# Windowed attention and a gated feed-forward in one kernel: sixteen steps ordered by hand instead of eleven, a bias added by TensorE, two decoding instructions a step

## The chip, the cores and the metric

One core of one Trainium2 chip. The metric is the device time of one execution in microseconds (us).

## The reference, cut to what matters

```python
# q, k, v: (4, 8, 768, 64) float32; n_global = 8, n_local = 96 (int64 inputs)
scores = (1 / sqrt(64)) * q @ k^T
keep   = (key < n_global) | (0 <= query - key < n_local)
dist   = n_local where a key is only global, else |query - key|
scores = where(keep, scores - slope[head] * dist, -1e9)      # slope = 2 ** -(head + 1)
x      = softmax(scores) @ v        # heads side by side: (4, 768, 512)
h      = relu(x @ w_in)             # w_in (512, 1024), float64
c      = h conv_w over 3 neighbours in the sequence
out    = (h * sigmoid(c)) @ w_out   # w_out (1024, 512), float64
```

The weights of the feed-forward arrive as float64 and are decoded on the chip from their two words.

## The kernel before, in words

**Attention.** A job is one batch, one half of the sequence (384 queries) and one pair of heads: 4 x 2 x 4 = 32 jobs of 3 steps of 128 queries, 96 steps. A step sees at most 232 keys (96 before it, its own 128, 8 global ones). `scores` (L371) multiplies q and k into PSUM. For jobs 0 to 8 (`NATIVE` = `BESIDE` = 9) these are float32 matmuls over 64 rows, and the two heads of the pair stand in rows 0 to 63 and 64 to 127; head 0 writes a tile `s`, head 1 a tile `sb` of another pool (banks m0, m1). From job 9 on q is split into a high and a low part (`prep`, L125) and both heads write one tile `s`. `maxima` (L403) adds the table of biases with one VectorE instruction a head, scales by -0.125 and takes the minimum; its result goes back into PSUM. `exps` (L418) is ScalarE's exponential with its sum, and a small ScalarE instruction (L431) that adds an offset to the sum. `normalise` (L433) is a step later: a reciprocal on VectorE, head 0 on GpSimd, head 1 on ScalarE while `s < SHARED`. `transposes` (L445), two steps later, turns the probabilities by TensorE and moves them out by ScalarE (L453). `values` (L456) multiplies a job's three steps by v, and `mixed` (L477) splits the result into xh (ScalarE, L481) and xl (VectorE, L482).

**Feed-forward.** `ffn(n)` (L647) lists the work of half a batch: `mm1` (x @ w_in, L489), `relu`, `conv` (one GpSimd and two VectorE instructions, L539), `gate`, `saturated`, `split`, and `mm2` (L604). It is queued when a half's four jobs are through (every 12 steps) and spread over the steps that follow.

**Decoding.** A piece of the weights is 512 words a partition; there are 16, w_in first. Each needs three VectorE instructions on its words (`weight_bits`, L310), a GpSimd cast (`weight_high`, L321) and one VectorE subtraction (`weight_low`, L326). `work` takes them off a list while a budget in us a step lasts; their listed costs are 0.35, 0.62, 0.62 and 0.56. `need` forces pieces that a matmul is about to read. A piece that has been read out frees the buffer of the load four pieces later.

**Order.** Steps 0 to `HAND` - 1 = 10 run in the program's order on every engine, with a few warm-up matmuls between (`WARM`). From step 11 on a scheduler orders each engine's instructions at build time from its own estimate of when operands and buffers come free. The eight PSUM banks are: two `s`, two for transposes, one for values, and m0, m1, m2.

The loop of the steps by hand (L774 on), before:

```python
scores(s)
if ends(s - LAG_V): values((s - LAG_V) // NB)
transposes(s - LAG_T)          # with ScalarE's eviction
maxima(s); exps(s); normalise(s - 1)
# tables of the next heads, warm-up matmuls
work("dve", budget)
if ends(s - LAG_V - 1): mixed((s - LAG_V - 1) // NB)
work("pool", 1.3)
# loads; prep of the next job where i == 0
```

Of the kernel before, what the change touches and what calls it, by code (L numbers as in the profile page):

```python
# [20 lines left out]
P = 128  # L21
# [14 lines left out]
NPB = 3  # L36
SHARED = 40
CHECK_EVERY = 3
HAND = 11
NATIVE = 9  # L40
BESIDE = 9
WARM = (43, 0, 12, 0, 0, 8, 8, 4, 4, 4, 4, 4)
WARM_INSIDE = (0, 0, 14, 8, 8)
EARLY = 1
DECODE_BY_HAND, DECODE_LATER = (0.3, 1.2, 1.4), (1.2, 1.2)
FIRST_LOADS = (0, 0, 1, 2)
SHARE = (0.3, 0.5)
AT = ((2, 4, 5, 9, 16, 25), (1, 2, 4, 6, 7, 12, 16))
# [18 lines left out]
def fast_path(tc, io):  # L67
# [49 lines left out]
    def load_v(m):  # L117
# [32 lines left out]
    load(0)  # L150
    load(1)

    turns = [0, 0]

    def bank(name, scores=False):
        s = cur.get("s", 0)
        own = (2,) if s < NB * BESIDE else (0,) if exact else (0, 1, 2)
        if scores:
            own = (0, 1)
        turns[scores] += 1  # L160
        k = own[turns[scores] % len(own)]
        return ps_m.tile([P, 512], F32, tag=f"m{k}", name=name)
# [208 lines left out]
    def scores(s):  # L371
        m, i = steps[s]
        b, u, hp = jobs[m]
        w = NKC[u]
        first = u == 0 and i == 0
        n, c0 = (W0, NPREV) if first else (WIN, 0)
        k0 = key_start(u, i)
        both = ps_s.tile([P, 2, 256], F32, tag="s", name=f"s{s}")
        sp = [both[:, 0], bank(f"sb{s}", True) if m < BESIDE else both[:, 1]]
        for j in range(2):  # L380
            if m < NATIVE:
                rq, rk = raw[m]
                r, a = (j * D, 0) if m < BESIDE else (0, j)
                last_mm[s] = T.matmul(  # L384
                    sp[j][:, c0 : c0 + n],
                    rq[r : r + D, a * TB + i * P : a * TB + (i + 1) * P],
                    rk[r : r + D, a * w + k0 : a * w + k0 + n],
                    start=True,
                    stop=True,
                )  # L390
                continue
            qh, ql, kk = qk[m]
            for n_, (q_, st, sp_) in enumerate(((qh, True, False), (ql, False, True))):
# [7 lines left out]
        st_s[s] = (sp, c0, n, first)  # L401

    def maxima(s):  # L403
        m, i = steps[s]
        b, u, hp = jobs[m]
        sp, c0, n, first = st_s[s]
        mm = p1.tile([P, 8], F32, tag="mm", name=f"mm{s}", bufs=6)
        for j in range(2):
            h = 2 * hp + j
            tb = tab[:, h, WIN:] if first else tab[:, h, 0:WIN]  # L410
            last_ttr[s] = V.tensor_tensor_reduce(  # L411
                out=sp[j][:, c0 : c0 + n], in0=sp[j][:, c0 : c0 + n], in1=tb,
                scale=-0.125, scalar=3.0e38, op0=ALU.add, op1=ALU.min,
                accum_out=mm[:, j : j + 1],
            )
        st_s[s] = (sp, c0, n, mm)
# [28 lines left out]
    def transposes(s):  # L445
        m, i = steps[s]
        pb, _, _, _ = st_s.pop(s)
        pt = ps_t.tile([P, 2, 2, P], F32, tag="t", name=f"t{s}")
        for j in range(2):
            for c in range(2):  # L450
                T.transpose(pt[:, j, c, :], pb[:, j, c * P : (c + 1) * P], ident)  # L451
        sb = p2.tile([P, 2, 2, P], F32, tag="pt", name=f"pt{s}", bufs=NB + 1)
        last_ev[s] = A.activation(sb, pt, AF.Copy)  # L453
        st_pt[s] = sb

    def values(m):  # L456
# [17 lines left out]
                    stop=c == 1,  # L474
                )

    def mixed(m):  # L477
# [4 lines left out]
        cur["mixed"] = V.tensor_tensor(xl, pv[m], xh.bitcast(F32), ALU.subtract)  # L482

    def ends(s):
        return s >= 0 and s % NB == NB - 1
# [285 lines left out]
    for s in range(len(steps) + LAG_V + 1):  # L771
        cur["s"] = s
        m, i = steps[s] if s < len(steps) else (len(jobs), -1)
        if s < HAND:  # L774
# [2 lines left out]
                values((s - LAG_V) // NB)  # L777
            if s < len(WARM_INSIDE):
                warm(WARM_INSIDE[s])
            if s >= LAG_T:  # L780
                transposes(s - LAG_T)
            maxima(s)
            exps(s)
            if s:
                normalise(s - 1)
            if i == 1 and m + 1 < NPAIR:
                table(2 * m + 2, X=G)
                table(2 * m + 3, X=G)
# [8 lines left out]
                conv_weights((s - 4) // 2)  # L797
            budget = DECODE_BY_HAND[min(s // 3, len(DECODE_BY_HAND) - 1)]
            work("dve", budget)
            if ends(s - LAG_V - 1):  # L800
                mixed((s - LAG_V - 1) // NB)
            work("pool", 1.3)
        else:
            if hand:
# [14 lines left out]
                    left += 1  # L819
                k = -(-sum(cost for cost, _, _ in queue) // left)  # L820
            if ends(e):
                mixed(e // NB)
            if s <= len(steps):
                normalise(s - 1)
            if s < LAG_V + SPU:
# [125 lines left out]
    def general_head(m, hp, i, j, qg, kg, vg, dist, mask, parts):  # L951
# [94 lines left out]
```

## Time and profile before

| what | us |
|---|---|
| three runs | 463.18, 462.77, 453.68 |
| median of the runs | 462.77 |
| the profiled execution | 452.65 |
| its span, first to last instruction | 450.73 |

| engine | busy us in the span |
|---|---|
| TensorE | 434.5 |
| VectorE | 351.9 |
| ScalarE | 304.0 |
| GpSimd | 225.8 |

Busy time is the sum of an engine's instructions in the profiled execution. The records call TensorE PE, its weight loads PEld, VectorE DVE, ScalarE ACT, GpSimd POOL; L411 is line 411 of the kernel. Times in a row count from the start of the span. Matmuls are pipelined and their ends are modelled, so that their spacing from start to start says more than their length.

### The profile page before, as it was taken

The numbers are of one execution on the slowest core, as the hardware profiler recorded it, in microseconds if no ns is written. First come the engines' busy times: TensorE is split into PE (matmuls) and PEld (weight loads), VectorE is DVE, ScalarE is ACT, GpSimd is POOL, SyncE is SP. The second block draws the span as 40 slices with busy tenths as digits, with TensorE's granted clock in tenths as the row PEclk, the third lists the DMA queues.
The fourth block names the chain that finished last, engine by engine and source line by source line (L and its number), as shares of the span: only waits on it lengthen the run. The fifth ranks groups of instructions, "written<-read, shape, count | busy, mean of one in ns | idle before, by whom it ended". The sixth has DMA issues, their size and how long they took to land.

```text
span 450.7 us, 9020 instructions
## 1 busy us (share of the span) xinstructions
PE 434.5 (96%) x3027; PEld 375.6 (83%) x3027; DVE 351.9 (78%) x927; ACT 304.0 (67%) x839; POOL 225.8 (50%) x315
## 2 busy tenths in 40 slices
PE   8789999999889999999999999999999999998997
PEld 6555678899768988899989988889989988798876
DVE  6899998889989877757989897847989986447800
ACT  3778878788799667647776576646775696547610
POOL 5654446637835472656675585646675651022000
PEclk9989999999999999999999999999999999999999
DMA  6979941343244332353234333442335223584111
GB/s 213 306 221 275 279 121 43 108 147 105 83 129 150 108 107 97 92 166 107 86 120 160 107 108 91 130 138 81 106 119 163 81 83 119 207 293 132 47 49 52
DMA packets 22662, 60.02 MB, mean 133 GB/s; under 512 B 3024, under 2 KB 5584, under 8 KB 22608
## 3 DMA queue, kind: packets, MB, share of 16 engines
q1 hardware_dynamic: 18992, 53.01, 38.1%
q10 hardware_dynamic: 3616, 6.36, 3.8%
q8 instruction: 26, 0.43, 0.4%
q14 instruction: 28, 0.23, 0.2%
HBM read 53.07 MB, written 6.29 MB: 132 GB/s over the span
## 4 chain that ended last, share of the span: by engine, by line
PE 73%; DVE 5%; ACT 4%; DMA 4%; POOL 2%; issue 2%; ACTq 0%; POOLq 0%; DVEq 0%
PE o L611 24%; PE h L500 24%; PE pv L469 7%; PE t L451 7%; PE s L394 6%; DMA check<-in_w 3%; DVE c L547 1%; PE last L632 1%; POOL pbuf L443 1%; PE sb L384 1%; PE s L384 1%; DVE c L548 1%; DVE c L599 1%; ACT pbuf L425 1%; ACT sat L577 1%
## 5 line engine op out<-in xcount | busy, mean ns | idle before, releaser
L443 POOL TENSOR_SCALAR pbuf<-pbuf,mm 128x232 f32<-128x232 f32 (+1 forms) x152 | 109.1, 726 | 74.1 <-DVE mm L437 49.2
L425 ACT ACTIVATE pbuf<-s,mm 128x232 f32<-128x232 f32 (+1 forms) x165 | 72.5, 444 | 37.6 <-DVE mm L411 22.8
L411 DVE CUSTOM_DVE_ANT_0 s<-s,tab 128x232 f32<-128x232 f32 (+1 forms) x165 | 63.1, 384 | 24.9 <-PE s L394 21.8
L546 POOL TENSOR_SCALAR c<-hbuf,cw 128x382 f32<-128x382 f32 (+1 forms) x64 | 50.0, 786 | 59.3 <-ACT hbuf L510 59.3
L611 PE MATMUL o<-woh,gh 128*128 128x512 f32 x184 | 74.0, 402 | 0.0
L611 PE MATMUL o<-wol,gh 128*128 128x512 f32 x184 | 73.2, 398 | 0.0
L611 PE MATMUL o<-woh,gl 128*128 128x512 f32 x184 | 73.2, 399 | 0.0
L451 PE MATMUL t<-ident,pbuf 128*128 128x128 f32 x384 | 63.0, 278 | 6.6 <-ACT pbuf L441 3.7
L453 ACT ACTIVATE pt<-t 128x512 f32<-128x512 f32 x96 | 58.0, 604 | 15.4 <-PE t L451 15.3
L451 PEld LDWEIGHTS t<-ident,pbuf 128*128 128x128 f32 x384 | 45.5, 141 | 19.6 <-ACT pbuf L441 5.1
L500 PE MATMUL h<-xh,wih 128*128 128x384 f32 x252 | 58.1, 345 | 1.7 <-ACT hbuf L510 1.2
L500 PE MATMUL h<-xl,wih 128*128 128x384 f32 x252 | 58.8, 342 | 0.0
L500 PE MATMUL h<-xh,wil 128*128 128x384 f32 x252 | 56.3, 340 | 0.0
L469 PE MATMUL pv<-pt,v 128*64 128x128 f32 (+1 forms) x768 | 50.0, 279 | 0.3 <-ACT pt L453 0.3
L469 PEld LDWEIGHTS pv<-pt,v 128*64 128x64 f32 (+1 forms) x768 | 42.3, 138 | 8.9 <-issue 2.5
L500 PEld LDWEIGHTS h<-xh,wih 128*128 128x128 f32 x252 | 42.9, 189 | 4.1 <-ACT hbuf L510 1.9
L547 DVE SCALAR_TENSOR_TENSOR c<-hbuf,cw,c 128x382 f32<-128x382 f32 (+1 forms) x64 | 43.7, 697 | 3.0 <-POOL c L546 2.7
L500 PEld LDWEIGHTS h<-xh,wil 128*128 128x128 f32 x252 | 44.2, 189 | 0.3 <-issue 0.3
L500 PEld LDWEIGHTS h<-xl,wih 128*128 128x128 f32 x252 | 44.0, 189 | 0.2 <-issue 0.2
L548 DVE SCALAR_TENSOR_TENSOR c<-hbuf,cw,c 128x382 f32<-128x382 f32 (+1 forms) x64 | 43.4, 686 | 0.3
L510 ACT ACTIVATE hbuf<-h 128x384 f32<-128x384 f32 x64 | 31.9, 500 | 17.4 <-PE h L500 17.0
L611 PEld LDWEIGHTS o<-woh,gl 128*128 128x128 f32 x184 | 34.7, 188 | 7.7 <-issue 0.2
(119 smaller groups left out, 846.6 us busy)
## 6 DMA issues: line engine op xcount, KB each, us to landing
v<-in_vv SPq DMA_DIRECT2D x32, 384.0 KB, 3.7
rq<-in_qk SPq DMA_DIRECT2D x23, 384.0 KB, 3.1
wr<-in_w SPq DMA_DIRECT2D x16, 512.0 KB, 5.2
check<-in_w SPq DMA_DIRECT2D x16, 512.0 KB, 4.6
rk<-in_qk SPq DMA_DIRECT2D x12, 504.0 KB, 3.6
out<-ob ACTq DMA_DIRECT2D x23, 256.0 KB, 2.1
rk<-in_qk SPq DMA_DIRECT2D x11, 408.0 KB, 3.2
rq<-in_qk SPq DMA_DIRECT2D x16, 96.0 KB, 4.4
```

The source lines that it names most:

```text
L411: last_ttr[s] = V.tensor_tensor_reduce(out=sp[j][:, c0 : c0 + n], in0=sp[j][:, c0 : c0 + n], in1=tb, scale=-0.125, scalar=3.0e38, op0=ALU. ...
L425: last_exp[s] = A.activation(pb[:, j, c0 : c0 + n], sp[j][:, c0 : c0 + n], AF.Exp, bias=mm[:, j : j + 1], scale=-1.0, accum_out=mm[:, 2 + ...
L443: G.tensor_scalar(x, x, inv, 1.0, ALU.mult, ALU.mult)
L451: T.transpose(pt[:, j, c, :], pb[:, j, c * P : (c + 1) * P], ident)
L453: last_ev[s] = A.activation(sb, pt, AF.Copy)
L469: T.matmul(pv[m][64 * j : 64 * j + 64, i * P : (i + 1) * P], vt[m][:n, i, c, 64 * j : 64 * j + 64], sb[:n, j, c, :], start=c == 0, stop=c ...
L500: T.matmul(ps[:, :TB], w_[:, k, fs], x_, start=part == 0 and k == 0, stop=part == 2 and k == NK - 1,)
L510: A.activation(half, ps[:, :TB], AF.Relu, scale=0.5)
L546: G.tensor_scalar(c, *tap(1), 1.0, ALU.mult, ALU.mult)
L547: V.scalar_tensor_tensor(c, *tap(0), c, ALU.mult, ALU.add)
L548: V.scalar_tensor_tensor(c, *tap(2), c, ALU.mult, ALU.add)
L611: last = T.matmul(ps, g_[:, f], w_[:, f], start=f == 0 and part == 0, stop=f == NF - 1 and part == 2,)
```

## The change

Steps 0 to 15 are ordered by hand instead of 0 to 10, in a new order: ScalarE's high half of the mixed heads comes ahead of the step's exponentials, its eviction of the transposes behind them, VectorE's low half ahead of the decoding. Jobs 1 to 12 (steps 3 to 38) are "biased": q is scaled by -0.125 beforehand, on GpSimd (in place for jobs 1 to 8, in place of the cast for 9 to 12), TensorE adds -0.125 times the table of biases to the scores by a matmul with a bf16 identity, one a head, and VectorE takes the minimum of both heads with one tensor_reduce. Jobs 0 to 8 have one PSUM tile of two banks for both heads, two of them; at job 9 this pool is given up for the old `s`, m0 and m1. The decoding budgets become 0.3 for steps 0 to 2, 0.9 for steps 3 to 15, and 1.2 later.

```diff
-HAND = 11
+HAND = 16
+BIASED = (1, 13)
-DECODE_BY_HAND, DECODE_LATER = (0.3, 1.2, 1.4), (1.2, 1.2)
+DECODE_BY_HAND, DECODE_LATER = (0.3, 0.9), (1.2,)
...
-    ps_s = pool("ps_s", 2, space=PSUM)
-    ps_m = pool("ps_m", 1, space=PSUM)
+    ps_m = {2: pool("ps_m", 1, space=PSUM)}
+    ps_w = tc.tile_pool(name="ps_w", bufs=2, space=PSUM)
+    wide = [ps_w, ps_w.__enter__()]
+    def narrow():
+        wide[0].__exit__(None, None, None)
+        ps = tc.tile_pool(name="ps_s", bufs=1, space=PSUM)
+        ps_s.append(ps.__enter__())
+        ps_m[0] = ps_m[1] = ps_s[0]
...
     def prep(m, part):
+        if m < NATIVE and biased(m) and part == 0:
+            q = raw[m][0][:, :TB]
+            G.tensor_scalar(q, q, -0.125, 1.0, ALU.mult, ALU.mult)
...
-            G.tensor_copy(qh, rq)
+            if biased(m):
+                G.tensor_scalar(qh, rq, -0.125, 1.0, ALU.mult, ALU.mult)
+            else:
+                G.tensor_copy(qh, rq)
...
-            V.tensor_tensor(ql, rq, qh.bitcast(F32), ALU.subtract)
+            if biased(m):
+                V.scalar_tensor_tensor(ql, rq, -0.125, qh.bitcast(F32), ALU.mult, ALU.subtract)
+            else:
+                V.tensor_tensor(ql, rq, qh.bitcast(F32), ALU.subtract)
...
+    A.activation(ident16, ident, AF.Copy, scale=-0.125)
...
-        both = ps_s.tile([P, 2, 256], F32, tag="s", name=f"s{s}")
-        sp = [both[:, 0], bank(f"sb{s}", True) if m < BESIDE else both[:, 1]]
+        if m < BESIDE:
+            both = wide[1].tile([P, 2, 512], F32, tag="s", name=f"s{s}")
+        else:
+            if not ps_s:
+                narrow()
+            both = ps_s[0].tile([P, 2, 256], F32, tag="s", name=f"s{s}", bufs=2)
+        sp = [both[:, 0], both[:, 1]]
+        def bias(j):
+            last_mm[s] = T.matmul(
+                sp[j][:, c0 : c0 + n], ident16, bias_of(s, j), start=False, stop=True
+            )
...
+            if biased(m):          # jobs 9 to 12, behind each head
+                bias(j)
+        for j in range(2 if m < NATIVE and biased(m) else 0):
+            bias(j)                # jobs 1 to 8, behind both heads
...
     def maxima(s):
+        if biased(m):
+            last_ttr[s] = V.tensor_reduce(
+                mm[:, 0:2], both[:, :, c0 : c0 + n], axis=mybir.AxisListType.X, op=ALU.min,
+            )
-        for j in range(2):
+        for j in range(0 if biased(m) else 2):
...
+            x = (s - LAG_V - 1) // NB if ends(s - LAG_V - 1) else None
             if s >= LAG_T:
                 transposes(s - LAG_T)
+            if x is not None:
+                mixed_high(x)
             maxima(s)
             exps(s)
+            if s >= LAG_T:
+                evict(s - LAG_T)
             if s:
                 normalise(s - 1)
+            if x is not None:
+                mixed_low(x)
...
             work("dve", budget)
-            if ends(s - LAG_V - 1):
-                mixed((s - LAG_V - 1) // NB)
             work("pool", 1.3)
```

## Rows read from the trace of the kernel before

**Rows 1.** Busy time by stage: stretch, its length, then for each engine its busy us and (instructions); last the granted clock of TensorE as a share of full, the share of the DMA engines, and GB/s.

```profile
11.75:46.04 34.29, 28.78 (x230) 19.60 (x227) 32.87 (x112) 26.71 (x94) 19.16 (x27) 0.95 0.93 268
46.04:82.00 35.96, 35.88 (x255) 27.81 (x255) 33.45 (x96) 28.33 (x89) 20.64 (x28) 1.00 0.52 159
82.00:140.00 58.00, 53.83 (x397) 47.44 (x398) 52.09 (x117) 49.05 (x141) 31.74 (x34) 1.00 0.34 109
140.00:430.00 290.00, 288.83 (x1962) 257.85 (x1961) 225.42 (x574) 193.05 (x502) 147.84 (x198) 1.00 0.38 121
```

**Rows 2.** VectorE in order of time, the first bias instruction of step 3 and of step 16: start us, length us, engine, line, operation, out<-in, shapes, count.

```profile
11.75 0.31 DVE L411 CUSTOM_DVE_ANT_0 s<-s,tab 128x136 f32<-128x136 f32 x1 [0.29 <-PE sb L384]
...
46.04 0.40 DVE L411 CUSTOM_DVE_ANT_0 s<-s,tab 128x232 f32<-128x232 f32 x1
```

**Rows 3.** The chain of waits between 42 and 82 us: shares of that stretch by line (the chain enters it at 44.74 us).

```profile
by line: PE h L500 33.3%; PE pv L469 14.7%; PE t L451 13.9%; PE sb L384 13.2%; PE s L384 13.0%; PE h L521 3.6%; ACT hbuf L510 1.3%; issue 0.2%
```

**Rows 4.** The chain of waits between 96 and 116 us, some of its pieces.

```profile
98.58 1.22 DVE c L599
...
100.69 3.13 DMA rq<-in_qk
...
105.69 1.41 POOL pbuf L443
```

**Rows 5.** VectorE in order of time, steps 7 and the start of 8.

```profile
24.11 0.40 DVE L411 CUSTOM_DVE_ANT_0 s<-s,tab 128x232 f32<-128x232 f32 x1
...
24.43 0.44 DVE L411 CUSTOM_DVE_ANT_0 sb<-sb,tab 128x232 f32<-128x232 f32 x1
...
24.78 0.16 DVE L437 RECIPROCAL mm<-mm 128x2 f32<-128x2 f32 x1
24.86 0.67 DVE L330 TENSOR_TENSOR wil<-w,wih 128x512 fp32r<-128x512 f32 x1
...
27.07 0.56 DVE L482 TENSOR_TENSOR xl<-pv,xh 128x384 fp32r<-128x384 f32 x1 [0.47 <-ACT xh L481]
```

**Rows 6.** VectorE's instructions by stage (busy us, count, then clock, DMA share, GB/s): first those that read the raw words (tile wr; the two stages), then those of line 330 (the low planes).

```profile
11.75:46.04 34.29, 17.44 (x28) 0.95 0.93 268
46.04:82.00 35.96, 12.77 (x18) 1.00 0.52 159
...
11.75:46.04 34.29, 5.56 (x8) 0.95 0.93 268
```

**Rows 7.** A short reduce on VectorE (groups by form: busy us, mean ns, idle before).

```profile
L358 DVE TENSOR_REDUCE misc<-misc 128x1 f32<-128x32 f32 x1 | 0.2, 178 | 0.0
```

**Rows 8.** TensorE in order of time: the warm-up matmuls (bf16, 128 columns) ahead of the next piece, and two of the score matmuls of a job with split q.

```profile
11.55 0.62 PE L169 MATMUL warm<-setup 128*128 128x128 bf16 x8
12.01 0.39 PE L451 MATMUL t<-ident,pbuf 128*128 128x128 f32 x2
...
86.11 0.27 PE L394 MATMUL s<-kk,qh 128*128 128x232 f32 x1
86.22 0.28 PE L394 MATMUL s<-kk,ql 128*128 128x232 f32 x1
```

**Rows 9.** TensorE in order of time: the scores of a step by hand, and those of a step that the scheduler ordered.

```profile
16.80 0.46 PE L384 MATMUL s<-rk,rq 64*128 64x232 f32 x1
16.81 0.46 PE L384 MATMUL sb<-rk,rq 64*128 64x232 f32 x1
...
17.40 0.33 PE L451 MATMUL t<-ident,pbuf 128*128 128x128 f32 x1
...
48.55 0.66 PE L384 MATMUL s<-rk,rq 64*128 64x232 f32 x2
49.14 0.66 PE L451 MATMUL t<-ident,pbuf 128*128 128x128 f32 x4
49.73 0.66 PE L384 MATMUL sb<-rk,rq 64*128 64x232 f32 x2
```

**Rows 10.** ScalarE in order of time, step 7.

```profile
24.57 0.60 ACT L453 ACTIVATE pt<-t 128x512 f32<-128x512 f32 x1 [0.53 <-PE t L451]
25.06 0.45 ACT L425 ACTIVATE pbuf<-s,mm 128x232 f32<-128x232 f32 x1
...
25.49 0.46 ACT L425 ACTIVATE pbuf<-sb,mm 128x232 f32<-128x232 f32 x1
...
26.07 0.29 ACT L431 ACTIVATE mm<-mm,misc 128x2 f32<-128x2 f32 x1
26.27 0.39 ACT L441 ACTIVATE pbuf<-pbuf,mm 128x136 f32<-128x136 f32 x1
26.57 0.47 ACT L481 ACTIVATE xh<-pv 128x384 fp32r<-128x384 f32 x1
```

**Rows 11.** GpSimd, groups by form: a scaling of 382 columns and a cast of 768.

```profile
L546 POOL TENSOR_SCALAR c<-hbuf,cw 128x382 f32<-128x382 f32 x32 | 24.3, 762 | 18.1 <-ACT hbuf L510 18.1
L137 POOL CAST qh<-rq 128x768 fp32r<-128x768 f32 x23 | 23.2, 1007 | 31.0 <-issue 13.2 <-PE s L394 9.3 <-DMA rq<-in_qk 8.4
```

**Rows 12.** Who waited for whom (us in total, times, longest): the first row of 11.75 to 46.04 us, and the first of 82 to 140 us.

```profile
ACT pt L453 <- PE t L451: 6.2, 10, 1.6
...
POOL qh L137 <- DMA rq<-in_qk: 8.4, 2, 7.1
```

**Rows 13.** The stretch from 20 to 30 us, columns as in Rows 1.

```profile
20.00:30.00 10.00, 8.22 (x74) 6.11 (x74) 9.42 (x30) 7.91 (x28) 5.98 (x8) 0.83 0.87 268
```

More of the change, by code (lines that the diff above doesn't have):

```diff
@@ L82, in fast_path @@
     pg = pool("pg", 4)
-    ps_s = pool("ps_s", 2, space=PSUM)
     ps_t = pool("ps_t", 2, space=PSUM)
     ps_v = pool("ps_v", 1, space=PSUM)
-    ps_m = pool("ps_m", 1, space=PSUM)
+    ps_m = {2: pool("ps_m", 1, space=PSUM)}
     p2 = pool("p2", 2)
+    ps_w = tc.tile_pool(name="ps_w", bufs=2, space=PSUM)
+    wide = [ps_w, ps_w.__enter__()]
+    ps_s = []
+    def narrow():
[3 more added lines that the diff above has]
+        ps_m[0] = ps_m[1] = ps_s[0]
+        pools.insert(len(pools) - 1, ps)
     jobs = [(b, u, hp) for b in range(B) for u in range(2) for hp in range(NPAIR)]
@@ L123, in load_v, with biased @@
         vt[m] = t
+    def biased(m):
+        return BIASED[0] <= m < BIASED[1]
     def prep(m, part):
+        if m < NATIVE and biased(m) and part == 0:
+            q = raw[m][0][:, :TB]
+            G.tensor_scalar(q, q, -0.125, 1.0, ALU.mult, ALU.mult)
         if m >= len(jobs) or m < NATIVE:
@@ L151, in fast_path, with bank @@
     load(1)
-    turns = [0, 0]
-    def bank(name, scores=False):
+    turns = [0]
+    def bank(name):
         s = cur.get("s", 0)
         own = (2,) if s < NB * BESIDE else (0,) if exact else (0, 1, 2)
[L158 to L162, printed above, removed]
+        turns[0] += 1
+        k = own[turns[0] % len(own)]
+        return ps_m[k].tile([P, 512], F32, tag=f"m{k}", name=name)
     queue, cur, exact = [], {}, []
@@ L192, in fast_path @@
     make_identity(nc, ident)
+    ident16 = const.tile([P, P], BF16, name="ident16")
     V.tensor_copy(rel, reli)
@@ L388, in scores @@
                     start=True,
-                    stop=True,
+                    stop=not biased(m),
                 )
@@ L392, in scores @@
             qh, ql, kk = qk[m]
-            for n_, (q_, st, sp_) in enumerate(((qh, True, False), (ql, False, True))):
+            for n_, (q_, st, sp_) in enumerate(((qh, True, False), (ql, False, not biased(m)))):
                 last_mm[s] = T.matmul(
@@ L400, in scores, with bias_of @@
                 )
-        st_s[s] = (sp, c0, n, first)
+            if biased(m):
+                bias(j)
+        for j in range(2 if m < NATIVE and biased(m) else 0):
+            bias(j)
+        st_s[s] = (sp, c0, n, both)
+    def bias_of(s, j):
+        m, i = steps[s]
+        b, u, hp = jobs[m]
+        if u == 0 and i == 0:
+            return tab[:, 2 * hp + j, WIN:]
+        return tab[:, 2 * hp + j, 0:WIN]
     def maxima(s):
@@ L405, in maxima @@
         b, u, hp = jobs[m]
-        sp, c0, n, first = st_s[s]
+        sp, c0, n, both = st_s[s]
         mm = p1.tile([P, 8], F32, tag="mm", name=f"mm{s}", bufs=6)
-        for j in range(2):
-            h = 2 * hp + j
-            tb = tab[:, h, WIN:] if first else tab[:, h, 0:WIN]
+        if biased(m):
[3 more added lines that the diff above has]
+        for j in range(0 if biased(m) else 2):
             last_ttr[s] = V.tensor_tensor_reduce(
-                out=sp[j][:, c0 : c0 + n], in0=sp[j][:, c0 : c0 + n], in1=tb,
+                out=sp[j][:, c0 : c0 + n], in0=sp[j][:, c0 : c0 + n], in1=bias_of(s, j),
                 scale=-0.125, scalar=3.0e38, op0=ALU.add, op1=ALU.min,
@@ L451, in transposes, with evict @@
                 T.transpose(pt[:, j, c, :], pb[:, j, c * P : (c + 1) * P], ident)
+        st_pt[s] = pt
+    def evict(s):
         sb = p2.tile([P, 2, 2, P], F32, tag="pt", name=f"pt{s}", bufs=NB + 1)
-        last_ev[s] = A.activation(sb, pt, AF.Copy)
+        last_ev[s] = A.activation(sb, st_pt[s], AF.Copy)
         st_pt[s] = sb
@@ L475, in block, with mixed_high @@
                 )
-    def mixed(m):
+    def mixed_high(m):
         xh = px.tile([P, TB], F32R, tag="xh", name=f"xh{m}")
@@ L481, in mixed, with mixed_low @@
         A.activation(xh, pv[m], AF.Copy)
-        cur["mixed"] = V.tensor_tensor(xl, pv[m], xh.bitcast(F32), ALU.subtract)
+    def mixed_low(m):
+        xh, xl = xt[m]
+        V.tensor_tensor(xl, pv[m], xh.bitcast(F32), ALU.subtract)
     def ends(s):
@@ L821, in fast_path @@
             if ends(e):
-                mixed(e // NB)
+                mixed_high(e // NB)
+                mixed_low(e // NB)
             if s <= len(steps):
@@ L832, in fast_path @@
                 transposes(s - LAG_T)
+                evict(s - LAG_T)
             fill(k - k0)
@@ L957, in general_head @@
         for c, (a, z) in enumerate(parts):
-            sp = ps_s.tile([P, 512], F32, tag="s", name=f"gs{t}_{c}")
+            sp = ps_s[0].tile([P, 512], F32, tag="s", name=f"gs{t}_{c}", bufs=2)
             T.matmul(
```

## The prediction

> **What bounds the kernel now.** I read the busy times by stage first [rows 1]. From 11.75 to 46.04 us, which are steps 3 to 15 (the first bias of step 3 starts at 11.75, that of step 16 at 46.04 [rows 2]), VectorE is busy 32.87 of 34.29 us, ScalarE 26.71, TensorE 28.78. That stage is VectorE's: 34.29 / 13 = 2.64 us a step. From 46.04 to 82 TensorE is busy 35.88 of 35.96 us. From 82 to 140 VectorE has 52.09 and ScalarE 49.05 of 58 us; from 140 to 430 TensorE has 288.83 of 290. A busy TensorE is not TensorE at its peak, so I checked with the chain of waits: from where it enters the second stage, at 44.74, to 82 it is TensorE's but for 1.5% of the stretch [rows 3], while between 97 and 116 us it goes through VectorE's gate products, the load of one rq and the scalings on GpSimd [rows 4]. After 140 us nothing of the change runs, so I carry that stage over as it is.
>
> What a hand-ordered step costs VectorE is read in its order of time [rows 5]: at step 7 the two bias instructions start at 24.11 and 24.43, the reciprocal at 24.78, so the pair takes 0.67 us, then the decoding follows from 24.86 on. Of these there are 28 at the word tile and 8 at the low plane in the stage, 17.44 + 5.56 = 23.0 us or 0.64 us each: two thirds of VectorE's time [rows 6].
>
> The sum is made against the profiled execution's own 452.65 us. That is 0.2% under the lowest of the three runs (453.68) and 10.1 us under their median (462.77, with 463.18 beside it); nothing in the trace says what those 10 us are. I forecast on the profiled execution's scale and price the other level as a case of its own.
>
> **The change, part by part.**
>
> *One reduce for two biases, and TensorE's bias.* Per step two biases with their accumulator reads go, 0.67 us from start to start. A reduce over 2 x 232 columns comes. The trace has none so long: bounded below by one 232-column bias, 0.40 us, above by two of them, 0.80 [rows 5]. The nearest reduce, 32 columns, took 0.18 us and has no accumulator read behind it [rows 7]. I take 0.57, near the middle, a gain of 0.10 a step, 36 steps, 3.6 us of VectorE in all. The Trainium skill, "VectorE: DVE Perf Modes", section "The perf-mode tier table", says that a reduce runs at one element a cycle wherever its input lies, and its section "Rules for kernel authors" calls it the slowest operation of the engine. With the page's 0.96 GHz and some 150 cycles of start an estimate for 464 columns is 0.64 us; by that the gain would shrink to 0.03 a step, which speaks for the first rival below, and no run so far shows it.
>
> TensorE gets two matmuls of 232 columns a step. Matmuls of 232 columns stand 0.11 us apart (86.11, 86.22) [rows 8], so 0.22 a step. Bounds: 0.06 each, the spacing of the 128-column bf16 warm-up (8 in 0.46 us) [rows 8], and 0.29, that of one pass of the 64-row scores (half of 0.59) [rows 9]. Below nothing it can't be, as it is added work. In steps 3 to 15 TensorE has slack, 28.78 of 34.29 us; in steps 16 to 26 it lies on the path, 11 x 0.22 = 2.4 us; in steps 27 to 38 beside other engines.
>
> *Two decoding instructions a step by hand.* With budgets 1.2 and 1.4 the steps took two or three; by 46.04 us 2 (the 48 on words less 28 and 18) + 28 + 8 = 38 of 64 were done [rows 6]. With 0.9 every step takes exactly two (no piece costs 0.9, every two do): 3 + 13 x 2 = 29. So 9 x 0.64 = 5.8 us of VectorE work leave the stage and must be paid after it.
>
> *The hand order.* Per step VectorE then needs 0.57 + 0.08 + 2 x 0.64 + 0.55 / 3 = 2.1 us. ScalarE is next: from start to start the eviction takes 0.49, the exponentials 0.43 and 0.58, the sum's offset 0.20, the normalising copy 0.30, and a third of 0.47 goes to the mixed heads, 2.2 us [rows 10]. TensorE has 28.78 / 13 + 0.22 = 2.43 by its busy time, which counts pipelined ends, so it is a little too high. GpSimd has 19.16 us and gains five scalings of q at 0.8 us [rows 11]: 1.8 a step. I take 2.40 a step, near TensorE: 13 x (2.64 - 2.40) = 3.1 us gained. Ends: 2.2, gain 5.7; 2.64, gain 0. The eviction behind the exponentials takes away a wait that cost ScalarE 6.2 us in ten pieces [rows 12]; what stands late next is the score matmul, which waits for its own buffer. The high half of the mixed heads goes ahead of the exponentials: it waits for values of the step before, which are done; queued behind it are both exponentials. Scaling q on GpSimd adds a wait for the rq load of the next job, with the normalising of the next step queued behind it and the transposes behind that; the loads are issued a job earlier, so I cost it at nothing.
>
> *Scores beside each other.* In hand steps the passes of the two heads start together: 16.80 and 16.81, and the next other matmul at 17.40: 0.60 us for all four passes. In the automatic steps they are mostly apart: 48.55 to 49.14 for one head, the other only from 49.73 on, each alone 0.59 [rows 9]. Before, the two heads have separate tiles with separate releases; the new tile holds both and is released once, so both should be ready together. In the chain between 42 and 82 us score pieces take 13.2 + 13.0% of 40 us, 10.5 us [rows 3], for 11 steps; at 0.59 a step they would take 6.5 at most. That is 4.0 gained and a little more where a step has only 136 columns; I take 4.1. Lower end nothing. Less the 2.4 of the bias: 1.7 gained.
>
> *What is paid back.* From 46.04 to 82 VectorE has 35.96 - 33.45 = 2.5 us free and gets 1.1 by the reduce; 5.8 us come in. About 2.2 are left over, and they land from 82 us, where VectorE's products are on the path [rows 4]; I take 2.0, ends 0 and 5.8. In steps 27 to 38 the reduce gives 12 x 0.10 = 1.2 there, but four casts of qh become scalings: a cast of 768 columns is 1.01 us, a scaling of 382 is 0.76, so at most 1.5 [rows 11] and 4 x 0.5 = 2.0 on GpSimd. The two cancel; ends -1.2 and +2.0. The subtraction for ql that also scales replaces one of the same width, 0; the bf16 identity is one short ScalarE instruction ahead of step 0, 0 to 0.4. The change of pools at job 9 makes one step wait for the last exponentials of the one before: 0 to 2 us, I take 0.2.
>
> Sum: -3.1 - 1.7 + 2.0 + 0.2 = -2.6, so 452.65 - 2.6 = 450.0 us.
>
> **The rivals.**
>
> *R1, given back.* The reduce costs as much as the pair, the scheduler still sets the heads apart, and the bias is paid in full: -3.1 + 2.4 + 3.3 (5.8 - 2.5) + 2.0 (the scalings, nothing against them) + 0.2 = +4.8, 457.5. For it: TensorE is the bound from 44.74 on [rows 3]. Against: one tile, one release. A change that only postpones decoding does not do what it says; this is that case too.
>
> *R2, the other level.* The gain is as forecast, but new runs lie where two of the three shown lie: 450.0 + 10.1 = 460.1. For it: the two runs. Against: the profiled execution and the third. The granted clock was 0.83 of full between 20 and 30 us [rows 13], that is 1.2 GHz for part of it, in a stretch where TensorE was busy 8.22 of 10 us; denser steps should make this rarer.
>
> *R3, slower.* GpSimd is the place: by hand its order is fixed, and in each of five jobs the scaling of q stands before the normalising. GpSimd's longest wait for an rq load was 7.1 us, later in the run [rows 12]. If loads come late, with the DMA engines at 0.93 of their time in that stage [rows 1], 4 us a job are 20 us with nothing gained: 452.65 + 20 = 473. It decides once an rq lands later than the step behind which it is scaled, one job ahead of its use. Against it: GpSimd is busy 19.16 of that stage's 34.29 us [rows 1], so that it can stand still for a third of it before the steps feel it.
>
> *R4, more.* ScalarE sets the hand steps (5.7 gained), heads fall together (1.7), nothing is left over of the decoding, and the load of rq in the chain [rows 4] is late no more, 3.1: 452.65 - 10.5 = 442.2.
>
> **How the numbers follow.** Forecast 0.42 (446 to 454), R1 0.24, R2 0.14, R3 0.10, R4 0.10. Predicted 450.0. The range 440 to 462 holds the forecast, R1, R2 and most of R4; what it leaves out is R3, the far edge of R4 and R2's, under 0.2. Two per cent of 462.77 is 9.3 us, about what a measurement of this kernel can tell from no change: faster is below 453.5. Forecast and R4 lie there but for 0.05 of the forecast's upper edge: 0.47. R1, R2 and that edge: 0.43. R3: 0.10.
>
> **What would show it.** Right: the first reduce of step 16 starts near 43 us; hand steps of 2.4 us with two decoding instructions in each; a reduce of 0.5 to 0.6 us; s passes of jobs 5 to 8 in pairs; bias matmuls 0.1 us apart. Wrong: GpSimd waiting for rq before 40 us (R3); s passes 0.6 us apart per head, and decoding past 90 us with VectorE in the chain (R1); a step 16 that starts at 46 us or later.

## The result, and the profile after

| | runs | median us | lowest to highest |
|---|---|---|---|
| before, beside it | 9 | 454.63 | 452.13 to 463.18 |
| after | 9 | 456.31 | 454.33 to 457.86 |

The ratio is 1.0073, with a 95% interval of 1.0049 to 1.0097: slower by 0.7%, inside 2%, where the forecast was 450.0, faster by 0.6%. The time lies in the predicted range, and the sign was wrong. (About one run of before in four took 462 to 465 us, at a lower granted clock; the ratios leave these out.) The profiled execution after is the slowest of its nine, 457.86 us with a span of 455.8, against 452.65 and 450.7 before: 5.2 us, of which part is TensorE's clock (0.983 of full on average after, 0.995 before).

The stages of the kernel after, columns as in [rows 1], and then the stretch from 10 to 20 us:

```profile
11.75:46.04 34.29, 30.97 (x289) 22.33 (x288) 27.28 (x67) 29.07 (x99) 20.31 (x31) 0.92 0.86 242
46.04:82.00 35.96, 33.37 (x259) 26.60 (x257) 31.83 (x61) 27.04 (x85) 22.68 (x29) 1.00 0.63 187
82.00:140.00 58.00, 52.53 (x370) 46.89 (x369) 51.73 (x78) 45.13 (x129) 32.60 (x33) 0.94 0.29 91
140.00:430.00 290.00, 288.67 (x1984) 257.76 (x1983) 229.53 (x583) 194.85 (x509) 154.66 (x200) 1.00 0.39 124
...
10.00:20.00 10.00, 9.38 (x68) 6.99 (x68) 6.73 (x23) 7.60 (x27) 7.12 (x12) 0.66 1.01 303
```

VectorE has become light in the steps by hand (27.28 of 34.29 us, 32.87 before). But TensorE, full from 46.04 to 82 before, now stands still for 2.6 us of that stage and for 5.5 of the next (4.2 before).

The first reduces of steps 3 and 16, which answer to [rows 2], and the chain of waits between 42 and 82 us, to [rows 3]:

```profile
12.93 0.44 DVE L453 TENSOR_REDUCE mm<-s 128x2 f32<-128x272 f32 x1 [1.12 <-PE s L409]
...
46.05 0.64 DVE L453 TENSOR_REDUCE mm<-s 128x2 f32<-128x464 f32 x1
```

```profile
by line: DMA rq<-in_qk 12.2%; ACT pbuf L471 7.2%; DVE mm L453 7.1%; DVE w L339 6.5%; DVE c L599 6.5%; PE s L417 4.4%; issue 4.4%; PE h L573 4.0%; POOL c L598 3.8%; PE t L497 3.7%; PE pv L518 3.7%; DVE c L600 3.4%; DVE w L341 3.4%; SPq L121 
```

Where the chain was TensorE's but for 1.5%, it now runs over loads, exponentials, reduces and decoding (L339, L341).

VectorE in order of time at step 7, which answers to [rows 5], and its instructions on the raw words by stage, to [rows 6]:

```profile
24.40 0.15 DVE L483 RECIPROCAL mm<-mm 128x2 f32<-128x2 f32 x1
24.47 0.54 DVE L534 TENSOR_TENSOR xl<-pv,xh 128x384 fp32r<-128x384 f32 x1
24.93 0.68 DVE L341 SCALAR_TENSOR_TENSOR w<-wr,w 128x512 int32<-128x512 int32 x1
25.53 0.72 DVE L337 TENSOR_SCALAR w<-wr 128x512 int32<-128x512 int32 x1
26.17 0.62 DVE L453 TENSOR_REDUCE mm<-s 128x2 f32<-128x464 f32 x1
26.71 0.15 DVE L483 RECIPROCAL mm<-mm 128x2 f32<-128x2 f32 x1
```

```profile
11.75:46.04 34.29, 13.20 (x21) 0.92 0.86 242
46.04:82.00 35.96, 12.78 (x20) 1.00 0.63 187
82.00:140.00 58.00, 3.79 (x7) 0.94 0.29 91
```

Two decoding instructions a step. Seven on the words now run wholly or in part behind 82 us; before there was none (28 + 18 and 2 ahead make the 48). The reduce takes 0.54 us from start to start (26.17 to 26.71).

TensorE in order of time, a step by hand and one that the scheduler ordered ([rows 8, 9]), and who waited for its bias matmul, in 11.75 to 46.04 and in 82 to 140 us:

```profile
24.58 0.66 PE L417 MATMUL s<-rk,rq 64*128 64x232 f32 x4
25.18 0.37 PE L409 MATMUL s<-tab,ident 128*128 128x232 bf16 x2
25.39 0.38 PE L497 MATMUL t<-ident,pbuf 128*128 128x128 f32 x2
...
47.41 0.66 PE L417 MATMUL s<-rk,rq 64*128 64x232 f32 x4
48.01 0.27 PE L409 MATMUL s<-tab,ident 128*128 128x232 bf16 x1
48.05 0.42 PE L573 MATMUL h<-xh,wih 128*128 128x384 f32 x1
48.31 0.27 PE L409 MATMUL s<-tab,ident 128*128 128x232 bf16 x1
```

```profile
DVE mm L453 <- PE s L409: 6.2, 7, 1.8
...
DVE mm L453 <- PE s L409: 3.9, 1, 3.9
```

All four score passes take 0.60 us and stand together also where the scheduler orders them; the two bias matmuls take 0.21. At 48 us the scheduler has put a feed-forward matmul between the two, and the one reduce waits for the second.

**Where the time went** is seen best by what holds TensorE. Each matmul is counted from its start to the next one's start, at most for its length; the rest is gap; from 11.75 us to the end of the profiled executions, in us. No view prints these sums; they are added up from the traces. The last four columns are experiments below:

| | before | after | a_split | s_decode | w_b6 | w_b6_decode |
|---|---|---|---|---|---|---|
| scores | 54.2 | 49.3 | 51.3 | 51.8 | 47.3 | 47.7 |
| bias matmuls | 0 | 6.7 | 7.2 | 8.2 | 3.3 | 3.4 |
| feed-forward | 273.5 | 274.7 | 274.7 | 276.1 | 275.0 | 272.8 |
| all other matmuls | 97.0 | 97.0 | 95.5 | 94.9 | 97.1 | 96.4 |
| gaps | 10.9 | 12.7 | 7.3 | 9.8 | 17.3 | 9.2 |
| sum | 435.6 | 440.4 | 436.0 | 440.8 | 440.1 | 429.4 |

After against before: scores -4.9, bias +6.7, gaps +1.8, feed-forward +1.2 (in part the lower clock, 0.94 between 82 and 140 us).

The same score passes and bias matmuls by steps, counted in the same way, with what the forecast had for them:

| steps | scores before | scores after | bias after | change | forecast |
|---|---|---|---|---|---|
| 3 to 15 | 10.2 | 8.1 | 3.2 | +1.1 | 0.22 a step, inside the 2.40 |
| 16 to 26 | 10.4 | 6.5 | 2.0 | -1.9 | -4.1 + 2.4 = -1.7 |
| 27 to 38 | 5.7 | 7.8 | 1.4 | +3.5 | 0 |
| 39 to 95 | 28.4 | 27.3 | 0 | -1.1 | 0 |

A matmul's start depends on its neighbours, so that a microsecond of such a sum is no finding by itself. The steps can be placed in time by their reciprocals on VectorE. Those of step 16, before and after:

```profile
52.61 0.16 DVE L437 RECIPROCAL mm<-mm 128x2 f32<-128x2 f32 x1
...
48.69 0.17 DVE L483 RECIPROCAL mm<-mm 128x2 f32<-128x2 f32 x1 [0.67 <-ACT mm L477]
```

It comes 3.9 us earlier. At step 20 the two kernels are level (66.82 before, 66.63 after), at step 25 the kernel after is 3.5 later (83.73, 87.27), and from step 39 on about 5. So the head start is used up between 49 and 67 us, and the loss proper arises behind that.

### The profile page after: what moved, and what is told of

It reads as the page before. It is cut to its first block, busy times and chain, and to the rows that moved or that the text cites. A ratio compares the mean times of both kernels' runs of the same rounds, so it can differ in the third digit from the quotient of the medians.

```text
span 455.8 us, 9069 instructions
## 1 busy us (share of the span) xinstructions
PE 436.5 (96%) x3099; PEld 379.2 (83%) x3099; DVE 351.0 (77%) x819; ACT 304.6 (67%) x840; POOL 236.9 (52%) x323
## 4 chain that ended last, share of the span: by engine, by line
PE 69%; DVE 14%; DMA 6%; ACT 6%; issue 2%; POOL 1%; SPq 0%; ACTq 0%; DVEq 0%; POOLq 0%
PE o L663 25%; PE h L552 20%; PE t L497 7%; PE pv L518 7%; PE s L427 6%; DMA check<-in_w 3%; DVE c L599 3%; DVE mm L453 2%; DVE c L600 2%; DMA rq<-in_qk 2%; ACT pbuf L471 1%; PE s L417 1%; PE last L684 1%; DVE w L339 1%; DVE w L341 1%
## 5 line engine op out<-in xcount | busy, mean ns | idle before, releaser
L489 POOL TENSOR_SCALAR pbuf<-pbuf,mm 128x232 f32<-128x232 f32 (+1 forms) x152 | 115.1, 767 | 75.2 <-DVE mm L483 58.5
L471 ACT ACTIVATE pbuf<-s,mm 128x232 f32<-128x232 f32 (+1 forms) x192 | 84.3, 446 | 52.3 <-DVE mm L457 22.8
L497 PE MATMUL t<-ident,pbuf 128*128 128x128 f32 x384 | 64.5, 282 | 8.0 <-ACT pt L502 3.8
L497 PEld LDWEIGHTS t<-ident,pbuf 128*128 128x128 f32 x384 | 47.6, 144 | 17.7 <-ACT pbuf L487 4.7
L457 DVE CUSTOM_DVE_ANT_0 s<-s,tab 128x232 f32<-128x232 f32 (+1 forms) x120 | 46.3, 387 | 19.7 <-PE s L427 17.0
L599 DVE SCALAR_TENSOR_TENSOR c<-hbuf,cw,c 128x382 f32<-128x382 f32 (+1 forms) x64 | 45.5, 720 | 6.1 <-POOL c L598 5.7
L518 PE MATMUL pv<-pt,v 128*64 128x128 f32 (+1 forms) x768 | 49.3, 276 | 0.0
L600 DVE SCALAR_TENSOR_TENSOR c<-hbuf,cw,c 128x382 f32<-128x382 f32 (+1 forms) x64 | 46.0, 721 | 0.4
```

The source lines that it names most:

```text
L457: last_ttr[s] = V.tensor_tensor_reduce(out=sp[j][:, c0 : c0 + n], in0=sp[j][:, c0 : c0 + n], in1=bias_of(s, j), scale=-0.125, scalar=3.0e3 ...
L471: last_exp[s] = A.activation(pb[:, j, c0 : c0 + n], sp[j][:, c0 : c0 + n], AF.Exp, bias=mm[:, j : j + 1], scale=-1.0, accum_out=mm[:, 2 + ...
L489: G.tensor_scalar(x, x, inv, 1.0, ALU.mult, ALU.mult)
L518: T.matmul(pv[m][64 * j : 64 * j + 64, i * P : (i + 1) * P], vt[m][:n, i, c, 64 * j : 64 * j + 64], sb[:n, j, c, :], start=c == 0, stop=c ...
L599: V.scalar_tensor_tensor(c, *tap(0), c, ALU.mult, ALU.add)
L600: V.scalar_tensor_tensor(c, *tap(2), c, ALU.mult, ALU.add)
```

## The experiments

Medians in us; the ratio is to the kernel before, run beside it, with its 95% interval. The medians of before there are 452.6 to 453.6.

**First: undo one part of the change each.**

```diff
 a_decode  (after)   -DECODE... = (0.3, 0.9), (1.2,)   +(0.3, 1.2, 1.4), (1.2, 1.2)
 a_nobias  (after)   -BIASED = (1, 13)                 +BIASED = (0, 0)
 a_noscale (after)   -G.tensor_scalar(q, q, -0.125, ...)  # and at qh, ql; identity 1, reduce max
                     +V.tensor_scalar(mm[:, 0:2], mm[:, 0:2], -0.125, ...)   # exp scale 0.125
 b_decode  (before)  -DECODE... = (0.3, 1.2, 1.4), (1.2, 1.2)   +(0.3, 0.9), (1.2,)
```

> The changed kernel with the decoding budgets of before (1.2 in steps 3 to 5, 1.4 in steps 6 to 15, so up to three decoding instructions a step). T1, the postponed decoding: the nine decoding instructions that left the hand-ordered stage (5.8 us of VectorE) are what is paid in 60 to 100 us; then decoding ends near 85 us instead of 100 and the time falls by 3 to 5 us, to 451 to 453. T2, the scaling of q on GpSimd that waits in order for its load: hardly changed, 455 to 457, or more, as loads of raw words crowd the loads of q. T3, the bias on TensorE: unchanged, 456.

a_decode: 456.0, 1.0066 (1.0034 to 1.0099). The old decoding back in its place gains nothing.

> The changed kernel with no job biased: the two VectorE bias instructions a head come back, no scaling of q, no bias matmul; hand order, wide tiles and decoding stay. T3: TensorE gets back 72 matmuls of 0.11 us and VectorE keeps its old cost: 452 to 453. T2: the waits for rq on GpSimd before 60 us are gone, 453. T1: VectorE has 0.1 us a step more to do with the same backlog, 456 to 459.

a_nobias: 456.5, 1.0092 (1.0065 to 1.0118). Without the bias on TensorE nothing is gained either.

> The changed kernel without the scaling of q: the identity is 1, the reduce takes the maximum of the unscaled biased scores, a VectorE instruction of two columns scales it by -0.125, and the exponential scales by 0.125. T2: GpSimd's waits for rq (4.5 us in 46 to 82 us) and the three loads in the chain between 31 and 56 us go, 452 to 454. T1 and T3: one small VectorE instruction more a step (36 x 0.08 us), 456 to 458.

a_noscale: 459.32, 1.0144 (1.0081 to 1.0207). Without the scaling GpSimd's wait for rq between 46 and 82 us (4.5 us in the kernel after) is gone, and nothing is gained. The run puts 36 small VectorE instructions in its place, which were expected to cost 2.9 us, so it excludes that the scaling costs clearly more than that, as the third rival had it, and not every smaller cost.

> The kernel before with the new decoding budgets alone (0.3, then 0.9 in steps 3 to 10; 1.2 later). T1: the hand-ordered steps get shorter by the decoding that leaves them, and it is paid later: 455 to 458, decoding ends past 90 us. T2 and T3: no change or a little faster, 451 to 453, since neither part is in it.

b_decode: 461.79, 1.0179 (1.0062 to 1.0296). On the kernel before, postponing the decoding alone costs. How much is less clear than the median says: two of the four executions had a mean granted clock of 0.970 and 0.974 (465.25 and 464.48 us), the other two 0.989 (458.63 and 459.09 us), where before took 453.8 to 455.3 us at 0.987 to 0.989. At like clock it is 4 to 5 us. So a part that costs alone is worth nothing when it is undone in the changed kernel: the parts don't add.

**Second: the scheduler's share, and what is left.**

```diff
 a_hand11               (after)   -HAND = 16   +HAND = 11
 a_hand11_decode        = a_hand11 with the old decoding
 a_hand11_decode_nobias = that with BIASED = (0, 0): left are the wide tile and the order in a step
 b_hand16               (before)  -HAND = 11   +HAND = 16
```

> The changed kernel with 11 steps by hand instead of 16; all else stays. T5, the scheduler's share: steps 11 to 15 by hand bring step 16 forward, but leave the scheduler a worse start; then 452 to 454. T6, a stage that can't use the head start (VectorE is full from 60 to 130 us whatever comes before): 455 to 457, step 16 near 51 us and step 40 at the same place as in the changed kernel. T1 again, the postponed decoding: fewer steps at the small budget, so less postponed, 453 to 455.

a_hand11: 458.24, 1.0137 (1.0109 to 1.0164). Five steps less by hand are no cure.

> The changed kernel with 11 steps by hand and the decoding budgets of before: what is left of the change is the bias on TensorE with one reduce, the scaling of q, the wide tiles and the order inside a step. T5: 452 to 454. T6: 454 to 457. If the bias part brings its 7 us of VectorE after all, under 451.

a_hand11_decode: 457.07, 1.0106 (1.0080 to 1.0131).

> The changed kernel with 11 steps by hand, the decoding budgets of before and no job biased: only the wide tiles of two banks (both heads in one tile) and the order inside the 11 steps are left of the change. T5 and T1: neither is in it, so as before, 452 to 453. T7, the wide tiles: one release for both heads makes the scheduler set the four score passes together and later, and costs by itself: 455 to 457.

a_hand11_decode_nobias: 454.68, 1.0055 (1.0034 to 1.0075). Its waits of TensorE between 70 and 100 us:

```profile
PE s L417 <- ACT pbuf L471: 3.3, 2, 2.1
PE s L427 <- ACT pbuf L471: 2.3, 1, 2.3
```

The first line is TensorE standing in front of the scores for the exponentials that read the wide tile. Before, TensorE had no such wait in that stretch. That made the tile a suspect. The second line is not the wide tile: it is the first score of step 27, where the pool changes at job 9, and c_order below, with a tile for each head, has it too (the first row is of a_hand11_decode_nobias, the second of c_order):

```profile
85.80 0.38 PE L427 MATMUL s<-kk,qh 128*128 128x136 f32 x1 [2.32 <-ACT pbuf L471]
...
88.34 0.33 PE L428 MATMUL s<-kk,qh 128*128 128x136 f32 x1 [1.83 <-ACT pbuf L475]
```

The forecast had 0.2 us for this change of pools. The kernel after has no such gap there, and no experiment takes the change of pools out by itself.

> The kernel before with 16 steps by hand in its old order and its old budgets (1.4 in steps 6 to 15). T5: slower by the same 3 us as the changed kernel, 455 to 457. T6: step 16 as before or later (2.6 to 2.9 us a step, VectorE full), 453 to 456. If hand steps alone were the gain, under 451.

b_hand16: 454.29, 1.0043 (1.0022 to 1.0064). Sixteen steps by hand in the old order cost a little.

**Third: the wide tile and the order in a step, apart.**

```diff
 c_wide    = a_hand11_decode_nobias with the old order in a step
 c_order   = a_hand11_decode_nobias with a tile for each head:
-            both = wide[1].tile([P, 2, 512], F32, tag="s", ...)
+            sp = [wide[1].tile([P, 512], F32, tag=t, ...) for t in ("s", "sb")]
 c_order16 = c_order with HAND = 16
 a_split   = after with a tile for each head, and a reduce of 232 columns for each
```

> The kernel before with one thing of the change: one tile of two banks for the scores of both heads (steps 1 to 35), in the old order inside a step, with no bias on TensorE, the old decoding and HAND = 11. With this and the new order together the time was 454.7. Theory W (the wide tile costs: it comes free only when the exponentials of both heads have read it, so TensorE stands): 454 to 455.5, and TensorE waits for the exponential in front of the scores. Theory O (the order inside a step costs): 452 to 453.3, as before.

c_wide: 454.65, 1.0035 (1.0011 to 1.0060).

> The kernel before with the other thing: the new order inside a step (exponentials ahead of the eviction, the high half of the mixed values ahead of the maxima, the low half behind the reciprocal), two tiles of one bank for the two heads, no bias on TensorE, the old decoding and HAND = 11. Theory W: 452 to 453.3, as before. Theory O: 454 to 455.5.

c_order: 452.87, 0.9989 (0.9963 to 1.0015). The order in a step costs nothing; against a_hand11_decode_nobias, which has the same order, the tile costs 1.8 by the medians, 3.0 by the ratios.

> As the last, with the order by hand to step 15. Theory W: the new order gains its head start and does not lose it to the tile, 451.5 to 453.5, and the step-16 reciprocal 2 us or more ahead of the kernel before. Theory O, or a stage from 46 us on that can't use any head start: 453.5 to 455.5, the head start gone by 100 us.

c_order16: 454.56, 1.0016 (0.9982 to 1.0050). The head start is there (step-16 reciprocal 50.87) and is gone by step 39.

> The changed kernel with a tile of its own for each head in steps 1 to 35, each reduced by itself (two reduces of 232 columns for one of 464), all else as changed. Theory W: each head's bank comes free by itself, 454 to 455. Theory O: the reduces cost and nothing is gained, 456 to 457.5.

a_split: 452.76, 0.9991 (0.9968 to 1.0013). That is 3.5 us better than after, and TensorE's gaps fall from 12.7 to 7.3. So far theory W, the tile, held; but with 5.6 us of head start at step 16 (47.04) the kernel should have come out ahead of before, and didn't. The bias and the decoding were still in it.

**Fourth: with a tile for each head, the decoding and the bias again.** Jobs 1 to 5 are steps 3 to 17, the steps by hand and two more.

```diff
 s_decode    = a_split with the old decoding
 s_b6        = a_split   -BIASED = (1, 13)   +BIASED = (1, 6)
 s_b6_decode = both
 s_b9_decode = s_decode  -BIASED = (1, 13)   +BIASED = (1, 9)
```

> The changed kernel with a tile for each head (452.8), and the decoding budgets of before. Theory D (the postponed decoding takes the head start back): 450 to 451.5. Theory B (the bias matmuls from 46 us on do): 452.3 to 453.5.

s_decode: 457.62, 1.0103 (1.0060 to 1.0146). Outside both expectations: with the decoding early, the split tile is no better than the wide one (a_decode, 456.0).

> The changed kernel with a tile for each head, and the bias on TensorE only for jobs 1 to 5, the steps by hand; jobs 6 to 12 add it on VectorE as before. Theory B: 46 bias matmuls less where TensorE is full, of 0.105 us each at most 4.4, of which half: 450 to 451.5. Theory D: 452.5 to 454, VectorE, which has the decoding still to do, gets the biases too.

s_b6: 453.19, 1.0005 (0.9983 to 1.0027).

> Both: a tile for each head, the bias on TensorE only for jobs 1 to 5, and the decoding of before. Theory B or D alone: as the one of the other two that is the faster. Both: 449 to 450.5. Neither, the stage from 46 to 140 us has no use for a head start: 452 to 453.5.

s_b6_decode: 451.49, 0.9972 (0.9944 to 1.0000). With the decoding early, taking the bias of jobs 6 to 12 off TensorE gains 6.1 us; with the decoding late (a_split to s_b6) nothing.

> A tile for each head, the old decoding, the bias on TensorE for jobs 1 to 8 (18 passes or so behind 46 us; with 4 it took 451.5, with 44 457.6). Theory B (each pass costs where TensorE is full): in between by the passes, 453 to 455. A layout that happens to be bad with jobs 9 to 12: 451 to 452.5; with jobs 6 to 8: 456.5 to 458.

s_b9_decode: 453.60, 1.0048 (1.0013 to 1.0083). By the profiles 44, 22 and 4 bias matmuls stand between 46 and 140 us in s_decode, s_b9_decode and s_b6_decode: 457.6, 453.6, 451.5. That is 6.1 us for 40, 0.15 each, where a pair takes 0.21. The step from s_decode to s_b9_decode, 4.0 us by the medians and 2.5 by the ratios, whose intervals overlap a little, takes off the 24 of jobs 9 to 12 alone, which are steps 27 to 38, where the forecast had put them at nothing. The edits also give the biases back to VectorE and change GpSimd's work: for jobs 9 to 12 a scaling becomes a cast again, for jobs 6 to 8 the scaling that waits for rq goes. So the 2.1 us between s_b9_decode and s_b6_decode can be either.

**Fifth: the wide tile again, as the change has it.**

```diff
 w_b6_decode (after)  -BIASED = (1, 13)  +BIASED = (1, 6)   and the old decoding
 w_b6        (after)  -BIASED = (1, 13)  +BIASED = (1, 6)
```

> The changed kernel (one tile for both heads) with the decoding of before and the bias on TensorE for jobs 1 to 5 alone. With a tile for each head this took 451.5. Theory W (the one tile costs wherever it is): 453 to 455. Against it: 451 to 452, the tile costs only in some layouts.

w_b6_decode: 448.17 (446.56 to 448.66, 5 runs), 0.9902 (0.9882 to 0.9923). It beats both kernels, before by 1.0% and after by 1.7% (through the ratios, 0.9902 and 1.0073), and theory W falls: the wide tile is better here than the split one. Its stages, its instructions on the raw words, and its chain from 82 to 140 us:

```profile
11.75:46.04 34.29, 29.54 (x288) 20.20 (x287) 33.12 (x77) 28.73 (x98) 23.67 (x33) 1.00 0.93 281
46.04:82.00 35.96, 34.15 (x251) 27.30 (x250) 35.78 (x92) 29.96 (x95) 23.44 (x30) 1.00 0.51 150
82.00:140.00 58.00, 55.58 (x412) 49.81 (x412) 51.03 (x119) 48.99 (x138) 27.02 (x33) 1.00 0.38 121
```

```profile
11.75:46.04 34.29, 17.72 (x30) 1.00 0.93 281
46.04:82.00 35.96, 11.88 (x18) 1.00 0.51 150
82.00:140.00 58.00, 0.00 (x0) 1.00 0.38 121
```

```profile
by line: PE h L552 31.1%; PE pv L518 10.3%; PE o L663 9.8%; PE s L427 9.0%; DVE c L599 8.3%; PE t L497 7.6%; DVE c L600 6.7%; DVE s L457 3.6%; issue 3.5%; ACT pbuf L471 2.5%; DVE kk L159 1.8%; DVE xl L534 1.6%; ACT sat L629 1.6%; DVE mm L45
```

> The changed kernel (one tile for both heads) with the bias on TensorE for jobs 1 to 5 alone and the new decoding. With a tile for each head this took 453.2. Theory W: 455 to 457. Against it: 452.5 to 454.

w_b6: 457.38, 1.0101 (1.0038 to 1.0164). With the wide tile, postponing the decoding costs 9.2 us when the biases of jobs 6 to 12 are VectorE's; some of it may go with the clock, 0.981 to 0.992 in these five executions and 0.996 to 1.0 in w_b6_decode's. TensorE gets 49.32 of 58 us:

```profile
82.00:140.00 58.00, 49.32 (x352) 43.35 (x351) 51.96 (x117) 43.46 (x124) 27.32 (x32) 0.94 0.30 93
```

The same chain, 82 to 140 us, of the kernel after:

```profile
by line: DVE c L599 14.4%; DVE c L600 10.9%; DVE mm L453 7.6%; DVE kk L159 6.2%; PE o L663 5.8%; ACT gh L653 4.9%; ACT pbuf L471 4.6%; ACT sat L629 4.6%; issue 4.5%; DVE gl L654 4.1%; DVE xl L534 3.5%; DVE ql L161 3.1%; DVE wol L352 3.1%; A
```

In w_b6_decode the six largest shares are TensorE's but one; after, the four largest are VectorE's, the reduce among them, and the low planes of the decoding (wol) are still in it.

**The two disputed parts side by side**, medians in us, sixteen steps by hand:

| | bias of jobs 6 to 12 on TensorE | on VectorE |
|---|---|---|
| wide tile, decoding early | 456.0 | **448.2** |
| wide tile, decoding late | 456.3 (after) | 457.4 |
| split tile, decoding early | 457.6 | 451.5 |
| split tile, decoding late | 452.8 | 453.2 |

With the decoding early the bias behind the steps by hand costs 7.8 and 6.1 us. With the wide tile a part of the 7.8 may be GpSimd's scaling for jobs 6 to 8: a_decode's chain between 46 and 82 us has the load of rq at 18.9%, w_b6_decode's has none of it, and no run takes the two apart there. With the decoding late, the bias costs nothing; that it then takes from VectorE what the decoding has brought is argued. With the wide tile either of the two parts alone costs 8 to 9 us and both together 8: undoing one shows nothing, as the first batch did. With a tile for each head it is otherwise: on top of the whole bias, postponing the decoding gains 4.9 us (457.6 to 452.8). That both engines are full there is seen in the stages (in w_b6_decode TensorE 55.58 and VectorE 51.03 of 58 us); that this is why the two prices don't add is argued from it.

## Why the prediction was wrong

**The hand order was right in its pace and short in sum.** From the reciprocal of step 6 to that of step 16 there are 24.29 us, 2.43 a step, forecast 2.40; before, 27.83, or 2.78. With the decoding early (w_b6_decode) it is 2.67: most of that head start is postponed decoding. The sign that I had set, the first reduce of step 16 near 43 us, failed, 46.05: step 3 began 1.2 us later, and at 10 to 20 us the granted clock was 0.66 of full, with stretches at 1.2 GHz, in this execution. The experiment w_b6 has the same steps by hand, and its clock was full there:

```profile
12.23 0.44 DVE L453 TENSOR_REDUCE mm<-s 128x2 f32<-128x272 f32 x1 [0.44 <-PE s L409]
...
44.42 0.64 DVE L453 TENSOR_REDUCE mm<-s 128x2 f32<-128x464 f32 x1
```

That is 2.48 us a step, against 2.64 before: 2.1 us gained of the 3.1. The exponential of step 16 started 2.3 us earlier after than before (47.36, 49.67).

**The reduce was right**: 0.54 us from start to start, forecast 0.57; 0.63 long. The Trainium skill, "VectorE: DVE Perf Modes", section "The perf-mode tier table", has one element a cycle for it; the estimate of 0.64 made with that page's clock and start agrees with the length. The row by form:

```profile
L453 DVE TENSOR_REDUCE mm<-s 128x2 f32<-128x464 f32 x29 | 18.3, 632 | 9.1 <-PE s L409 9.0
```

Its idle time is what I had not priced: 9.0 us of waiting for the bias matmul. VectorE's bias instructions of the same steps had waited some 4 us for the scores.

**Scores beside each other was right**: -3.9 in steps 16 to 26, forecast -4.1, and with the bias there -1.9, forecast -1.7. It goes with the wide tile: these scores take 6.3 to 7.9 us in the kernels with it, 7.8 to 10.5 in those with a tile for each head.

**The failed step is TensorE's bias in steps 27 to 38, which I put at nothing, "beside other engines".** I took 0.22 a step and counted it for steps 16 to 26 alone, 2.4 us; measured there 2.0. In steps 27 to 38 the scores with their bias take 9.2 us of TensorE in the kernel after, where the scores alone took 5.7. It is so in all twenty traces: 8.2 to 9.2 us in the seven kernels with the bias there, 5.7 to 7.4 in the thirteen without. In time, 4.0 us go (2.5 by the ratios) when these 24 matmuls go while the decoding is early (s_decode to s_b9_decode). Between 82 and 140 us I had read VectorE's 52.09 as the bound and TensorE's 53.83 of 58 as slack [rows 1]; 4.2 us of gap was no cover for that. With the decoding late, as the change has it, taking the bias off alone gains nothing; so in the changed kernel the price is shown only together with the next one.

**The second failed step is "what is paid back", 2.0 us.** I subtracted VectorE's 2.5 free microseconds from the backlog of 5.8 as if the scheduler could fill them. No run has a price of its own for the postponed decoding: it costs 4 to 5 us on before, 9.2 and 1.7 on the two kernels with the bias on TensorE for jobs 1 to 5 alone, 0.3 on top of the whole bias with the wide tile, and gains 4.9 there with a tile for each head. The two parts undone together, on the wide tile, give 8.1 us, more than the change lost. From the reciprocal of step 16 to that of step 25 the kernel after takes 7.5 us longer than before; TensorE's gaps in that stretch are 4.5 us, 0.1 before, and 8 more feed-forward matmuls fall into it. Why the gaps are so long is not shown.

**The rivals.** The first, 457.5, came nearest (456.31): its sign, decoding past 90 us with VectorE in the chain, is what the trace shows. Two of its reasons were wrong: the heads do stand together, and the reduce is cheaper than the pair; and its 2.0 from step 27 on stood for GpSimd's scalings, not for the bias. So its nearness is in part luck. The third (GpSimd waiting for rq before 40 us) did not come: the two waits lie between 46 and 82 us, and a_noscale gains nothing. The second, a level near 460, did not show in the nine executions after. That denser steps should make the lower clock rarer is not shown: between 10 and 20 us the kernel after kept TensorE busy 9.38 of 10 us, at 0.66 of the full clock. The fourth, 442.2, did not come.

**What stays open.** The sign of the wide tile: it costs 1.8 (c_order), 3.5 and 4.2 us (late decoding), and gains 1.6 and 3.3 (early decoding, sixteen steps by hand). From step 16 on a scheduler lays the instructions out anew for each kernel, and layouts of the same work may differ by some us; no run here separates that from the tile, or from the bias and the decoding. So the 448.2 is shown for that kernel, not for each of its parts.

## What to carry to other kernels

When work is moved out of a stage, price it in the stage where it arrives, on every engine that is over 0.9 busy there, and put it at nothing only with a row that shows room: here 24 matmuls "beside other engines" made TensorE's scores some 2 us longer. If undoing single parts shows nothing, undo them in pairs: with the wide tile each of two parts hid the other's cost, and the version without both was 1.7% faster than the change.

## What the runs showed of the hardware

The kernel before took 450.9 to 454.0 us at a mean granted clock of 0.995 to 1.0, 453.4 to 455.3 at 0.987 to 0.992, and 462.4 to 465.5 at 0.959 to 0.970. So the 10 us that I could not name go with stretches at TensorE's lower level, 1.2 GHz; no trace of such an execution of before was kept. w_b6_decode had 0.996 to 1.0 in all five executions; what decides when the clock falls is not shown here.

Two bf16 bias matmuls of 232 columns took 0.21 us behind four 64-row score passes of 0.60. VectorE's products of the convolution, the same 128 instructions, took 87.1 us before and 91.5 after by their rows, so that most of what the one reduce saved VectorE (74.0 us of bias instructions before; 67.6 of bias instructions and reduces after) was lost; why they slowed was not tried.
